# First two chunk pairs of a state-space scan in half chunks of 64 tokens, and the loads and row products that go with it

## The chip, the cores and the metric

The kernel runs on one core of one Trainium2 chip. The metric is the device time of an execution in microseconds, smaller being better. TensorE (PE) multiplies matrices, VectorE (DVE), ScalarE (ACT) and GpSimd (POOL) do the elementwise work, SyncE (SP) issues nearly all transfers. PE's weight loads are listed apart as PEld, the queue of an engine's issued transfers with a q (SPq).

## The reference

A Mamba-2 scan (batch 4, 8 heads, 768 tokens, head size D = 32, state size N = 16) is followed by a two-layer block with a PReLU. In exact arithmetic the chunk length doesn't matter, and the kernel chooses its own.

```
for each chunk of the sequence:
    cum = cumsum(log a);  L[i, j] = exp(cum_i - cum_j), i >= j
    y = ((C B^T) * L) x  +  (C state) * exp(cum)
    state = exp(sum log a) * state + sum_j exp(cum_end - cum_j) B_j x_j
x2 = y as (3072 tokens, 256)
h = x2 @ w_in                                  # 256 x 2048
g = max(h, 0) + alpha * min(h, 0)
out = g @ w_out                                # 2048 x 256
```

`w_in` and `w_out` come as 64-bit floats, all else as 32-bit floats.

## The kernel before

**Tiling.** A pair `gp` is two chunks of 128 tokens of one batch row with all 8 heads: twelve pairs, three to a batch row. Four chunks (two pairs) are a group of 512 tokens, `xts[g]`, on which the two layers work. Group 0 is special: `first_two` runs pairs 0 and 1, then `hidden_two(0, f, t0, hp)` multiplies blocks f and f+1 of w_in by one half of the group's tokens, and from f = 4 on a loop runs `hidden(0, f)`, `output(f - 4)` and the steps of the next pairs (`ssm(2)`, `ssm(3)`), each a stage of the generator `pair(gp)`. The later groups run in `quad` and the like; nothing in them is changed.

**Weights.** They come in pieces of 512 KB (`raw`), in the order w_in 0, 1, 2, w_out 0, w_in 3, w_out 1, w_in 4, w_out 2, and so on in turn. Each is converted in four steps: `convert_a` (ACT twice, then POOL `wt` L267), `sign` (DVE L286), `convert_b` (DVE L296) and the add on POOL (L318). `convert_next` ends the conversion of the next piece and issues the load of the piece that is six further: the three calls in `first_two` issue pieces 6, 7 and 8.

**Pairs 0 and 1 before.** The decays of a chunk are made by a scan: PE spreads a row of `a` over 128 partitions (`spread_rows` L499, `spread` L511), DVE scans it against an identity (L908, L855), and the product with the gram of B and C (`gram_of` L822, `times` L851, on DVE or, through a copy by ACT, on POOL) is the weight by which x is multiplied (`outputs`, L870 and L878). `added` (L831) makes a chunk's contribution to the state, the state follows on DVE (L937, L968), `mask` on POOL (L838) spreads it for PE. `xT` is copied out of PSUM by ACT (L883).

**Row products.** `a` of half the batch is loaded as 96 rows of 128 tokens. `rows_scan` makes the products from each token to the chunk's end, `rows_turn` turns them over on PE for `pair_loads` (bn), `rows_out` stores the clamped rows (`z`) and the running products (`pf`) in DRAM. `ap` of a pair is loaded back from `pf` with each row repeated over partitions (L177, L223). Pair 2's state (L613) and its cd (L653, POOL) read pair 2's `ap`; its scans (L538) read `abc`, which is loaded from `z` (L160).

**Order.** It is written out by hand: `tc.manual_schedule` names all five engines, and each takes its instructions, SP its transfers, in the order of the program. A transfer's consumer, and a later transfer that reads what it stored, waits for its semaphore.

Of the kernel before, what the change touches and what calls it, by code (L numbers as in the profile page):

```python
# [9 lines left out]
F32 = mybir.dt.float32  # L10
# [12 lines left out]
def kernel(  # L23
# [25 lines left out]
    nc = tc.nc  # L49
# [112 lines left out]

    def load_pair(gp, decays=True):
# [8 lines left out]
        if gp == 0:  # L172
            load_a(ap, b, c)
        elif gp >= NB:
            rows = scratch["pf", b // 2].rearrange("(b h c) t -> b h (c t)", b=2, h=H)
            rows = rows[b % 2, :, c * Q : (c + 2) * Q]
            nc.sync.dma_start(out=ap, in_=rows.unsqueeze(1).to_broadcast([H, N, 2 * Q]))  # L177
# [42 lines left out]
    def load_second():  # L220

        rows = scratch["pf", 0].rearrange("(b h c) t -> b h (c t)", b=2, h=H)
        nc.sync.dma_start(out=loads["p", 1][3], in_=rows[0, :, 2 * Q : 4 * Q].unsqueeze(1)  # L223
                          .to_broadcast([H, N, 2 * Q]))
# [98 lines left out]
    def keep_warm(to, n, cols=2 * Q):  # L323

        for i in range(n):
# [6 lines left out]
    ident_h = const.tile([P, H * Q], F32, name="ident_h")  # L332
    nc.vector.tensor_copy(out=ident_h.rearrange("p (h t) -> p h t", h=H),
                          in_=ident.unsqueeze(1).to_broadcast([P, H, Q]))
# [17 lines left out]
    nc.vector.memset(ends[:, Q - 1 :], 1.0)  # L352

# [35 lines left out]
    def identity_bank():  # L389


        m5_bank.append(bank(3))
        nc.scalar.copy(out=m5_bank[0][:, HT:], in_=ident_h[:, :HT])
        ident_p.append(m5_bank[0][:, HT:])
# [15 lines left out]

    def rows_clamp(i):
        rows = loads.pop(("r", i))
        d0 = prep.tile([RW, SQ], F32, name="r0")
        nc.vector.tensor_scalar(out=d0[:, :Q], in0=rows, scalar1=1e-6, scalar2=1.0,
                                op0=ALU.max, op1=ALU.min)
        if i:
            nc.vector.tensor_scalar(out=d0[:, Q + 1 :], in0=rows[:, HQ + 1 :], scalar1=1e-6,
                                    scalar2=1.0, op0=ALU.max, op1=ALU.min)
        held[i] = d0
# [11 lines left out]
    def rows_out(i):  # L431


        d0 = held.pop(i)[:, : SQ if i else Q]
# [7 lines left out]

    def rows_turn(i, pr):

        ps = ss_tile() if i else ps_s.tile([P, 512], F32, name="ss")
        nc.tensor.transpose(ps[:, :RW], pr, ident[:RW, :RW])
        if i == 0:
            nc.tensor.transpose(ps[:, RW : RW + NF], al_n, ident[:NF, :NF])
        else:
            nc.tensor.transpose(ps[:, RW : 2 * RW], held["prs"], ident[:RW, :RW])  # L450
        t = bat.tile([P, RW], F32, name="prt")
        if i == 0:
            nc.scalar.copy(out=t, in_=ps[:, :RW])
        for v in range(2 if i else 0):
# [6 lines left out]
        if i == 0:  # L461
# [3 lines left out]
    def pair_loads(gp):  # L465
# [8 lines left out]
        else:  # L474
            pj = prt[i].rearrange("p (b h c) -> p b c h", b=2, h=H)[:, bi, c : c + 2]
# [6 lines left out]
    def first_a(ap, eng):  # L482

        z = prep.tile([P, 2, Q], F32, name="z", bufs=2)
        eng.memset(z[:, :, :1], 0.0)
        eng.tensor_scalar(out=z[:, :, 1:], in0=ap.rearrange("p (k t) -> p k t", k=2)[:, :, 1:],
                          scalar1=1e-6, scalar2=1.0, op0=ALU.max, op1=ALU.min)
        return z

    def spread_rows(z):  # L490

        ts = [bank(r) for r in range(4)]
        for k in range(2):
            for e in range(2):
                for r in range(4):
                    rs = slice(32 * r, 32 * r + 32)
                    row = 32 * r + N * e
                    cs = slice((2 * k + e) * Q, (2 * k + e + 1) * Q)
                    nc.tensor.matmul(ts[r][:, cs], ident[rs, row : row + 1].to_broadcast([32, P]),  # L499
                                     z[rs, k], start=(k == 0 and e == 0), stop=True,  # L500
                                     tile_position=(32 * r, 0), skip_group_check=True)
        return ts

    def spread(z, k, tile=lambda w: ss_tile()):

        ts = [tile(w) for w in range(2)]
        for q in range(4):
            for w in range(2):
                rs = slice(64 * w, 64 * w + 64)
                row = 64 * w + N * q  # L510
                nc.tensor.matmul(ts[w][:, q * Q : (q + 1) * Q],  # L511
                                 ident[rs, row : row + 1].to_broadcast([64, P]), z[rs, k],
                                 start=(q == 0), stop=True, tile_position=(64 * w, 0),
                                 skip_group_check=True)
        return ts
# [276 lines left out]
    def first_two():  # L792


        nat0, _, xt0, ap0 = loads["p", 0]

        dec = [work.tile([P, 2, H, Q], F32, name="dec") for i in range(2)]
        first = dec[0].rearrange("p a b t -> p (a b t)").rearrange(
            "p (r c) -> p r c", r=4)
        by_bank = first.rearrange("p r (k e t) -> p r k e t", k=2, e=2)  # L800
        pf0 = prep.tile([P, Q], F32, name="pf")
        new = {}

        def turned(nat, tp):
# [5 lines left out]
            nc.scalar.copy(out=bc.rearrange("p i t -> p (i t)"), in_=tp)  # L810
            cz = czp.tile([P, 2, 2, Q], F32, name="cz")
            for e in range(2):
                nc.scalar.mul(cz[:, e].rearrange("p k t -> p (k t)"),
                              bc[:, 2:].rearrange("p k t -> p (k t)"), par[:, e : e + 1])
            return bc, cz

        def gram_of(bc, cz, banks):
            gram = [t.rearrange("p (k h t) -> p k h t", k=2, h=2) for t in banks]
            for k in range(2):
                for r in range(4):  # L820
                    rs = slice(32 * r, 32 * r + 32)
                    nc.tensor.matmul(gram[r][:, k].rearrange("p h t -> p (h t)"), bc[rs, k],  # L822
                                     cz[rs, :, k], start=True, stop=True,
                                     tile_position=(32 * r, 0), skip_group_check=True)
            return gram

        def added(dps, bn, xt):
            for k in range(2):
                for r in range(4):
                    rs = slice(32 * r, 32 * r + 32)  # L830
                    nc.tensor.matmul(dps[rs, k], bn[:, k, rs],  # L831
                                     xt[:, k, 2 * r * D : 2 * (r + 1) * D],
                                     start=True, stop=True, tile_position=(0, 32 * r),
                                     skip_group_check=True)

        def mask(sm, new, ks):
            n = ks.stop - ks.start
            nc.gpsimd.tensor_tensor(  # L838
                out=sm.rearrange("p k (g m) -> p k g m", g=2),
                in0=new[:, ks].unsqueeze(2).to_broadcast([P, n, 2, 2 * D]),  # L840
# [3 lines left out]
        def copied(gram):  # L844
            g0 = op.tile([P, GT], F32, name="o_sb").rearrange("p (k h t) -> p k h t", k=2, h=2)
            nc.scalar.copy(out=g0, in_=gram)
            return g0

        def times(i, r, gram, eng=nc.vector):
            o = dec[1][:, :, 2 * r : 2 * r + 2] if i else by_bank[:, r]  # L850
            eng.tensor_tensor(out=o, in0=gram, in1=o, op=ALU.mult)  # L851

        def decays(k, w, t):
            ws = slice(512 * w, 512 * w + 512)
            nc.vector.tensor_tensor_scan(out=dec[1][:, k].rearrange("p h t -> p (h t)")[:, ws],  # L855
                                         data0=t, data1=ident_h[:, ws], initial=0.0,
                                         op0=ALU.mult, op1=ALU.add)

        def outputs(i, tiles, st, cd, xt, ws, warm=0):
            y = [t[:, : 2 * Q].rearrange("p (k t) -> p k t", k=2) for t in tiles]  # L860
            keep_warm(y[ws[0]].rearrange("p k t -> p (k t)"), warm)
            begun = False
            for k in range(2):
                if st[k] is None:
                    continue
                for q in range(4):
                    qs = slice(32 * q, 32 * q + 32)
                    for w in range(KC):
                        hs = slice(64 * w, 64 * w + 64)
                        nc.tensor.matmul(y[w][qs, k], st[k][hs, qs], cd[hs, k],  # L870
                                         start=not begun, stop=False,
                                         tile_position=(64 * w, 32 * q), skip_group_check=True)
                begun = True
            for w in ws:
                for k in range(2):
                    for q in range(4):
                        h = 4 * w + q
                        nc.tensor.matmul(y[w][32 * q : 32 * q + 32, k],  # L878
                                         xt[:, k, h * D : (h + 1) * D],
                                         dec[1][:, k, h] if i else by_bank[:, h // 2, k, h % 2],  # L880
                                         start=False, stop=True, tile_position=(0, 32 * q),
                                         skip_group_check=True)
                nc.scalar.copy(out=xts[0][:, w, 2 * i * Q : 2 * (i + 1) * Q],  # L883
                               in_=y[w].rearrange("p k t -> p (k t)"))

        def bn_of(gp):
# [585 lines left out]
```

## Time and profile before

| what | us |
|---|---|
| median of 3 runs | 358.47 (358.37 to 358.62) |
| the profiled execution | 358.36, its span 356.6 |
| first matmul of `hidden_two(0, 0, 0)` | 17.74 |
| first matmul of `hidden_two(0, 0, 2 * Q)` | 24.76 |
| `hidden(0, 4)` | 28.69 |
| PE busy | 349.9 (98%) |
| DVE, ACT, POOL busy | 240.4, 174.1, 205.3 |

The profile is one execution; its times count from the span's start. In a line of a timeline stand the start, the length, the engine, the line of the kernel, the instruction, output and inputs, the shapes, and in brackets how long the engine had been idle before and what ended that. The chain lists what the end waited for, in order of time.

### The profile page before, as it was taken

To read this page: it belongs to the slowest core of one execution; us is meant where nothing else is said; L and a number is where in the kernel's file an instruction comes from. 1 tells how busy PE (TensorE), PEld (TensorE's weight loads), DVE (VectorE), ACT (ScalarE), POOL (GpSimd) and SP (SyncE) were. 2 spreads that over 40 slices of the span, in tenths; PEclk is the share of its full clock that TensorE was granted. 3 is DMA by queue.
4 is the path that set the end of the run, shared out by engine and by line. 5 is a ranking of instruction groups with operands and counts; after the bars stand their busy time and mean duration, and the time that the engine had idled before them with its cause. 6 is when DMAs were issued, how large, how long until landed. Compare 5 with 4: busy or idle time off the path is not lost.

```text
span 356.6 us, 7560 instructions
## 1 busy us (share of the span) xinstructions
PE 349.9 (98%) x2894; PEld 288.3 (81%) x2894; DVE 240.4 (67%) x467; ACT 174.1 (49%) x387; POOL 205.3 (58%) x221
## 2 busy tenths in 40 slices
PE   8799999999999999999999999999999999999995
PEld 7576666578888888888888888888888888888885
DVE  6988986998748856857747856757856633643463
ACT  3577666535355346345345445345445344443431
POOL 4887568589938855725646626637526535434520
PEclk9999999999999999999999999999999999999999
DMA  7999999408355404403513513522001002002102
GB/s 115 188 195 328 289 249 226 121 16 167 93 96 124 98 2 75 104 2 75 94 41 74 91 48 68 92 51 61 13 4 29 0 2 31 0 0 32 29 1 62
DMA packets 105469, 30.19 MB, mean 85 GB/s; under 512 B 79880, under 2 KB 101336, under 8 KB 105432
## 3 DMA queue, kind: packets, MB, share of 16 engines
q1 hardware_dynamic: 105048, 29.52, 38.2%
q8 instruction: 23, 0.38, 0.4%
q10 hardware_dynamic: 384, 0.18, 0.2%
q14 instruction: 14, 0.11, 0.1%
HBM read 26.32 MB, written 3.37 MB: 83 GB/s over the span
## 4 chain that ended last, share of the span: by engine, by line
PE 95%; POOL 1%; DMA 1%; SPq 1%; issue 0%; ACT 0%; DVE 0%; POOLq 0%
PE bank L1108 33%; PE hp L1133 29%; PE bank L1034 8%; PE hp L996 6%; PE ss L1133 6%; PE hp L1011 2%; PE ss L758 1%; PE ss L702 1%; PE bank L1101 1%; PE ss L750 1%; DMA nat<-in_C_dram 1%; PE ss L776 1%; PE ss L713 1%; PE bank L511 1%; PE ss L589 1%; PE ss L768 0%
## 5 line engine op out<-in xcount | busy, mean ns | idle before, releaser
L1190 POOL TENSOR_TENSOR gt<-gt 128x512 f32<-128x512 f32 x58 | 74.1, 1278 | 21.1 <-DVE gt L1118 16.3
L1108 PE MATMUL bank<-gt,w_out 128*128 128x256 f32 x320 | 83.5, 381 | 0.0
L1108 PEld LDWEIGHTS bank<-gt,w_out 128*128 128x128 f32 x320 | 60.1, 190 | 9.2 <-issue 1.0
L1118 DVE SCALAR_TENSOR_TENSOR gt<-hp,s_mul,gt 128x256 f32<-128x256 f32 x96 | 42.0, 479 | 29.1 <-ACT gt L1116 26.9
L1180 POOL TENSOR_TENSOR gt<-gt 128x512 f32<-128x512 f32 x20 | 25.4, 1269 | 62.7 <-DVE gt L1118 56.0
L1116 ACT ACTIVATE gt<-hp,s_alpha 128x256 f32<-128x256 f32 x96 | 40.4, 472 | 34.5 <-PE hp L1133 31.4
L1108 PE MATMUL bank<-gt,ws 128*128 128x256 f32 x224 | 55.9, 379 | 0.0
L1108 PEld LDWEIGHTS bank<-gt,ws 128*128 128x128 f32 x224 | 42.3, 190 | 5.6
L1133 PE MATMUL hp<-xs,w_in 128*128 128x256 f32 x160 | 41.9, 384 | 0.0
L1133 PE MATMUL hp<-xs,ws 128*128 128x256 f32 x160 | 41.2, 380 | 0.0
L1159 DVE TENSOR_TENSOR hp<-hp,u 128x512 f32<-128x512 f32 x20 | 14.0, 700 | 35.2 <-ACT u L1157 35.2
L1133 PEld LDWEIGHTS hp<-xs,ws 128*128 128x128 f32 x160 | 30.3, 190 | 4.3 <-POOL xs L1075 0.2
L1133 PEld LDWEIGHTS hp<-xs,w_in 128*128 128x128 f32 x160 | 29.7, 190 | 4.5
L1034 PE MATMUL bank<-w_out,gt 128*128 128x256 f32 x128 | 31.0, 384 | 0.0
L1034 PEld LDWEIGHTS bank<-w_out,gt 128*128 128x128 f32 x128 | 23.6, 190 | 6.5 <-issue 2.9
L1133 PE MATMUL ss<-xT,w_in 128*128 128x256 f32 x96 | 24.6, 379 | 0.0
L996 PE MATMUL hp<-xT,w_in 128*128 128x512 f32 x48 | 22.7, 596 | 0.1
L616 POOL TENSOR_TENSOR sm<-state,bmask 128x256 f32<-128x256 f32 (+1 forms) x10 | 6.2, 618 | 28.9 <-DVE state L613 28.9
L532 DVE TENSOR_TENSOR_SCAN dec<-abc,bank 128x192 f32<-128x192 f32 x48 | 22.7, 523 | 0.0
L1148 ACT COPY m<-hp 128x512 f32<-128x512 f32 x8 | 4.7, 587 | 35.7 <-PE hp L1133 35.7
L1157 ACT COPY u<-hp 128x512 f32<-128x512 f32 x20 | 11.7, 586 | 19.4 <-PE hp L1133 19.4
L1167 DVE TENSOR_TENSOR c<-hp,m 128x512 f32<-128x512 f32 x20 | 13.8, 691 | 10.0 <-PE hp L1133 9.9
(204 smaller groups left out, 624.7 us busy)
## 6 DMA issues: line engine op xcount, KB each, us to landing
abc<-z SPq DMA_DIRECT2D x24, 192.0 KB
raw<-in_moe_w_in_dram SPq DMA_DIRECT2D x8, 512.0 KB
raw<-in_moe_w_out_dram SPq DMA_DIRECT2D x8, 512.0 KB
abc<-z SPq DMA_DIRECT2D x8, 512.0 KB
out_dram<-o_sb SPq DMA_DIRECT2D x32, 64.0 KB
nat<-in_B_dram SPq DMA_DIRECT2D x26, 64.0 KB
nat<-in_C_dram SPq DMA_DIRECT2D x24, 64.0 KB
xt<-in_x_dram SPq DMA_DIRECT2D x12, 128.0 KB
```

The lines of the kernel that those rows point to most:

```text
L532: nc.vector.tensor_tensor_scan(out=dv[:, o : o + SQ], data0=abc[k][:, s : s + SQ], data1=ident_p[0][:, :SQ], initial=0.0, op0=ALU.mult, op ...
L996: nc.tensor.matmul(hp, w_in[:, k, f * P : (f + 1) * P], xts[g][:, k], start=(k == 0), stop=(k == KC - 1))
L1034: nc.tensor.matmul(pos[0][t // 2][:, t % 2], gt[:, t * Q : (t + 1) * Q], w_out[:, f], start=(f == 0 and t % 2 == 0), stop=(f == NF - 1), s ...
L1108: nc.tensor.matmul(ms[g][i][:, h], w, blocks[g, z][n][:, p], start=(q == 0 and h == 0), stop=(q == NQ - 1), skip_group_check=True)
L1116: nc.scalar.mul(o[:, p], h[:, p], s_alpha[:, fs[p]])
L1118: nc.vector.scalar_tensor_tensor(out=o[:, p], in0=h[:, p], scalar=s_mul[:, fs[p]], in1=o[:, p], op0=ALU.mult, op1=ALU.max)
L1133: nc.tensor.matmul(to[:, p], w(2 * z + p), b, start=start and p == 0, stop=True, skip_group_check=True)
L1157: nc.scalar.copy(out=u2, in_=A)
L1159: nc.vector.tensor_tensor(out=Y, in0=Y, in1=u2, op=ALU.add)
L1167: nc.vector.tensor_tensor(out=c22, in0=A, in1=m5, op=ALU.add)
L1180: nc.gpsimd.tensor_tensor(out=tc_, in0=g22, in1=g12, op=ALU.subtract)
L1190: eng.tensor_tensor(out=o, in0=x0, in1=x1, op=ALU.subtract)
```

## The change

Pairs 0 and 1 are handled as four chunks of 64 tokens each, two to a half of the partitions, so the scans and products are over 256 elements and not 512, with tiles of 32x64 on PE. A chunk's state is made and masked one at a time. Pair 1's steps are put among the matmuls of `hidden_two(0, 2, 0)` by a function that is called after each. The copies out of y go half to ACT and half to DVE. A set of row products for chunks of 64 (`rows_short`) is made first and stored as `short`, from which pair 1's `ap` comes. The products for chunks of 128 come at the end of `first_two` (`rows_scan`, `rows_products`, then `load_products` of pair 2's `ap`, then `rows_turn`), and `load_pair(2)` no longer loads that `ap`. The `z` store, with its clamps now on POOL, follows pair 1's loads.

```diff
+    def load_products(gp, ap):
+        b, c = divmod(2 * gp, CPB)
+        rows = scratch["pf", b // 2].rearrange("(b h c) t -> b h (c t)", b=2, h=H)
+        rows = rows[b % 2, :, c * Q : (c + 2) * Q]
+        nc.sync.dma_start(out=ap, in_=rows.unsqueeze(1).to_broadcast([H, N, 2 * Q]))
     def load_pair(gp, decays=True):
...
-        elif gp >= NB:
-            rows = scratch["pf", b // 2].rearrange("(b h c) t -> b h (c t)", b=2, h=H)
-            rows = rows[b % 2, :, c * Q : (c + 2) * Q]
-            nc.sync.dma_start(out=ap, in_=rows.unsqueeze(1).to_broadcast([H, N, 2 * Q]))
+        elif gp > NB:
+            load_products(gp, ap)
...
     def load_second():
-        rows = scratch["pf", 0].rearrange("(b h c) t -> b h (c t)", b=2, h=H)
+        rows = scratch["short", 0].rearrange("(b h c) t -> b h (c t)", b=2, h=H)
...
+    def clamp(eng, out, in_):
+        eng.tensor_scalar(out=out, in0=in_, scalar1=1e-6, scalar2=1.0, op0=ALU.max, op1=ALU.min)
+    def rows_products():
+        d0 = held.pop(0)
+        rpf = prep.tile([RW, Q], F32, name="rpf")
+        nc.vector.tensor_tensor_scan(out=rpf, data0=d0[:, :Q], data1=zeros[:RW], initial=1.0,
+                                     op0=ALU.mult, op1=ALU.add)
+        scratch["pf", 0] = dr.tile([RW, Q], F32, name="pf0")
+        nc.sync.dma_start(out=scratch["pf", 0], in_=rpf)
...
+    def rows_short(r, rows):
+        clamp(nc.vector, starts_r[:RW, ::HQ], rows[:, ::HQ])
+        nc.vector.memset(r[:, ::HQ], 0.0)
+        pr = lent[3][:RW, 2]
+        nc.vector.tensor_tensor_scan(out=pr[:, ::-1], data0=r[:, 1:][:, ::-1],
+                                     data1=ends_q[:RW, ::-1], initial=0.0, op0=ALU.mult,
+                                     op1=ALU.add)
+        rpf = lent[3][:RW, 3]
+        nc.vector.tensor_tensor_scan(out=rpf, data0=r[:, :Q], data1=starts_r[:RW], initial=0.0,
+                                     op0=ALU.mult, op1=ALU.add)
...
     def first_two():
...
+        def spread(z, ts):
+            for e in range(2):
+                for r in range(4):
+                    rs = slice(32 * r, 32 * r + 32)
+                    row = 32 * r + N * e
+                    for j, hs in enumerate(halves):
+                        o = ts[r][hs, : 2 * Q].rearrange("p (k e t) -> p k e t", k=2, e=2)
+                        nc.tensor.matmul(o[:, :, e], ident[rs, row : row + 1]
+                                         .to_broadcast([32, HQ]), z[rs, :, hs], start=e == 0,
+                                         stop=True, tile_position=(32 * r, HQ * j),
+                                         skip_group_check=True)
+        def scan(i, r, t):
+            nc.vector.tensor_tensor_scan(out=dec[i][:, r], data0=t[:, : 2 * Q], data1=ident_q,
+                                         initial=0.0, op0=ALU.mult, op1=ALU.add)
...
+        def times(i, r, t):
+            nc.vector.tensor_tensor(out=dec[i][:, r], in0=t[:, 2 * Q :], in1=dec[i][:, r],
+                                    op=ALU.mult)
...
+        def copy_out(i, y):
+            for w in range(KC):
+                o = xts[0][:, w, 2 * i * Q : 2 * (i + 1) * Q].rearrange(
+                    "p (k j t) -> p j k t", k=2, j=2)
+                nc.scalar.copy(out=o[:, 0], in_=y[w][0])
+                nc.vector.tensor_copy(out=o[:, 1], in_=y[w][1])
...
+        nc.sync.dma_start(out=scratch["short", 0], in_=held.pop("short"))
         load_pair(1)
         load_second()
...
+        rows_clamp(0)
+        rows_out(0)
         load_next(2)
         load_pair(2, False)
         load_next(2)
         load_spread(2, *divmod(4, CPB))
...
+        convert_next()
+        convert_a(*pieces[1])
         xts[0] = xtp.tile([P, KC, GT], F32, name="xT")
+        copy_out(0, y)
+        sign(*pieces[1])
+        convert_b(*pieces[1])
+        prelu_of = {0: hidden_two(0, 0, 0, spare())}
+        for r in range(4):
+            scan(1, r, sp[r])
+        bn1 = pair_loads(1)
         convert_next(first=False)
+        mask(0, slice(3, 4))
+        own = [ss(), ss()]
+        bc1, cz1 = turned(nat1, own[0], nc.scalar)
...
+        added(dps, bn1, xt1)
+        cd1 = decayed_c(bc1, pf1)
+        def among(i, k):
+            if (i, k) == (0, 1):
+                states(1, dps, pf1)
+                gram_of(bc1, cz1, sp)
+                one_at_a_time(1, range(3))
+                for r in range(4):
+                    times(1, r, sp[r])
+                prelu_of[0]()
+                convert_a(*pieces[2])
+                sign(*pieces[2])
+            if (i, k) == (1, 0):
+                y = places(own, [bank(0), bank(1)])
+                x_products(y, xt1, 1)
+                state_products(y, 1, cd1)
+                copy_out(1, y)
+        prelu_of[2] = hidden_two(0, 2, 0, spare(), among)
+        convert_next(first=False)
+        mask(1, slice(3, 4))
         slope_signs()
+        prelu_of[2]()
+        pr = rows_scan(0)
+        rows_products()
+        load_products(NB, loads["p", NB][3])
+        rows_turn(0, pr)
```

In `hidden_two` the ACT part of the PReLU (L1017) moves into the function that it returns where t0 is 0.

## The prediction

> **What bounds the kernel now.** I read the busy tenths in 40 slices first, then the chain that ended last in order of time, then the timeline from 0 to 56 us engine by engine, SyncE's queue (SPq) included.
>
> ```profile
> PE   8799999999999999999999999999999999999995
> DVE  6988986998748856857747856757856633643463
> DMA  7999999408355404403513513522001002002102
> ```
>
> TensorE (PE) is full from the third slice on, so a microsecond won or lost in front of it is won or lost at the end, unless PE waits somewhere later. The DMA engines are full in the first seven slices, to about 60 us, and VectorE (DVE) nearly so. The chain says where the full stretch starts:
>
> ```profile
> 24.33 0.38 ACT xT L883
> 24.71 0.04 issue
> 24.76 3.80 PE hp L1011 x16
> 28.56 0.13 issue
> 28.69 1.95 PE hp L996 x4
> ```
>
> At 24.76 pair 1's xT lies in SBUF and the two `hidden_two(0, ..., 2 * Q)` start; from there no link but PE follows. All that the change does in front counts by how it moves 24.76, called T1. All that it moves behind T1 counts by what it makes PE wait for. Three places of the timeline show how little room there is behind T1: SPq, DVE, and the conversion of w_out that `output(4)` needs.
>
> ```profile
> 31.84 0.41 SPq L249 DMA_DIRECT2D raw<-in_moe_w_in_dram  x1
> 32.36 0.41 SPq L249 DMA_DIRECT2D raw<-in_moe_w_out_dram  x1
> ```
> ```profile
> 35.29 0.75 DVE L1000 SCALAR_TENSOR_TENSOR gt<-hp,s_mul,gt 128x512 f32<-128x512 f32 x1
> 35.95 0.27 DVE L613 SCALAR_TENSOR_TENSOR state<-state,ap,ss 128x64 f32<-128x64 f32 x1
> 36.14 2.41 DVE L538 TENSOR_TENSOR_SCAN dec<-abc,bank 128x256 f32<-128x256 f32 x4
> ...
> 44.22 0.69 DVE L296 SCALAR_TENSOR_TENSOR wr<-wt,wr 128x512 uint32<-128x512 uint32 x1
> ```
> ```profile
> 45.00 1.27 POOL L318 TENSOR_TENSOR w_out<-wr,wg 128x512 uint32<-128x512 uint32 x1 [1.16 <-DVE wr L296]
> ...
> 46.41 1.90 PE L1034 MATMUL bank<-w_out,gt 128*128 128x256 f32 x8
> ```
>
> L613 is pair 2's state and reads `ap`, the products of pair 2. Today `ap` is loaded at 17.15, so L613 never waits. From L613 to L296 at 44.22 DVE has no gap over 0.2 us; GpSimd (POOL) waits for that L296, and PE takes the result 0.14 us after POOL's 46.27. So a delay of L613 reaches PE at `output(4)`, less some 0.1 us.
>
> **What the Trainium skill says.** "PSUM — Partial Sum Buffer", section "Engine vs sequencer instructions": the queues of ScalarE, VectorE and GpSimd are strict FIFO; a late L613 holds all behind it. The trace agrees: starts follow the program's order. "DMA: Bandwidth & Descriptors", section "Two DMAs through the same engine are not ordered": a transfer that reads what another wrote must be issued after a wait for the first one's semaphore, so the issuing queue stands. The same page, "Anatomy of one DMA", gives a fixed part of about 2.0 us, most of it the receipt of the last byte. Here: issued into an idle queue, the first `ap` took from 0.79 to 3.73, when DVE used it, 2.9 us; raw piece 1 had its last packet at 12.52 and ScalarE (ACT) began it at 13.25, 0.7 us later. "TensorEngine Tiling (Array Packing)", section "Available Configurations": 32x64 tiles are eight at once. The later half pairs agree: L702's 64 records ran in 0.84 us, while L713's 32x128 tiles took 1.08.
>
> **The front, part by part.** The setup (two 64x256 identity copies for one of 128x1024 at 0.77, four memsets) lies beside `keep_warm`, which holds PE to 4.58 while z is done at 4.07; without that cover it costs up to 0.5. The store `short` is ready on DVE at about 5.3 and SPq comes to it at 7.5; `load_second` waits for its landing near 13.5, and SPq is there at 15; the z store needs POOL's clamps, done by 9.5. So SPq stands nowhere new in front. DVE: eight scans of 512 (4.57 us at L908, 4.8 at L855) become eight of 256 at 0.60 (L538), -4.6. The products with the gram, five on DVE at 0.68 and three on POOL (1.28, 1.77, 1.29) with ACT copies of 0.59, become eight on DVE at 0.35 (half of 0.68): DVE -0.6, POOL -4.3, ACT -1.8. Added on DVE: four more L968-like states at 0.28 (1.1), two more row scans (0.42 + 0.40), four copies out of y at about 0.25 (half of an ACT 0.37, plus start). Added on POOL: masks one by one at 0.46 to 0.63 (eight instructions against three, +2.5) and three row clamps, 1.2 by L486's 1.06 for 254 elements. PE: spreads 1.59 and 2.06 become about 0.9 and 0.65, each gram 1.1 becomes 0.65; `added` at L589's 0.45 is level.
>
> Pair 0, in order: spread done at 5.6; scans to 8.0; cz and pf0 on DVE to 8.9; gram done at 9.2; products and states to 11.7; POOL's three masks end at 11.8. Then w_in piece 0: ACT 11.3 to 12.0, POOL 12.6, DVE 13.3, POOL's add (1.27) 14.6. `copy_out` stands on ACT behind `convert_a` of piece 1, whose data comes at 13.25 as today: 13.25 + 0.68 + 0.67 + 2 x 0.28 = 15.15. So the first `hidden_two` starts at **15.2 instead of 17.74**.
>
> Pair 1: `hidden_two` 1.95 and transposes 0.65 to 17.8; ACT's four copies (0.37, 0.45, 0.45, 0.37) to 19.5; `added` to 18.7 (xt's last packet is at 17.13); two matmuls of the next `hidden_two`, then gram at 20.3. POOL: cd (0.73) 20.3, three masks 22.1. DVE: products 20.3 to 21.7. So the state products end at 22.6, `hidden_two` at 23.1, xT is ready by 23.6: 1.2 before T1. But `rows_turn(0)` stands on PE before the next `hidden_two`, and its `pr` comes from a DVE scan behind `convert_b` (to 24.3), two `rest` (0.44 each, to 25.2), a memset and the scan (0.48): 25.6, and **T1 becomes about 25.9, +1.1 us**. Its uncertainty is about -2.5 to +1 us, since each engine's order was worked out by hand. Without that transpose T1 would be 23.4, -1.4.
>
> **The products of pair 2.** This is what I expect to decide. `ap` of pair 2 leaves SPq at 17.15 and comes back at the end of `first_two`, behind a store of `pf`. Ahead of that store on SPq stand the raw loads of the three `convert_next`: pieces 6, 7, 8, of 512 KB, issued at 27.41 to 32.25. In the trace's DMA packets the queue is served in that order: abc of pair 2, then piece 6 from 32.97, piece 8's last packet at 37.50. The early `ap` falls out (its packets lay among nat's from 20.79), -0.4: 37.1. Then:
> - `pf`'s 96 packets: 0.2, 37.3.
> - Its receipt, a store to DRAM, which no row shows: not under the 0.7 of a load, hardly over the skill's 2.0; I take 1.0, 38.3. SPq stands from 32.3 on; behind it wait pieces 9 to 11 and pair 3's loads.
> - `ap`: 0.6 us of issue, landing 2.9 to 3.3 after its start. The lower is the first `ap`; for the upper, another `ap` into an idle queue was issued at 79.06 with its last packet at 81.41, plus 0.7 to 1. **41.4**, between 40.4 and 42.6.
>
> L613 waits for it: 41.4 against 35.95 (36 to 37 with T1 moved), so DVE is 5.5 us behind today. Nothing takes it up: behind L613 come 9.0 us of work to L296's end at 44.91, and DVE is full. POOL stands too: cd (L653) reads `ap`. PE: the gram of pair 2 needs a bank that L1000 (39.59) frees, now at 45.8 instead of 40.3; `output(4)` needs POOL's add, at 51.7 instead of 46.27. PE is delayed by 5.5 - 0.1 to 0.2 = 5.3. The front's +1.1 or -1.4 is **contained in this, not added**: PE waits there until a time that the transfers set. The later pieces come some 3 us later, which a PE 5.3 later doesn't feel.
>
> The sum is made against 358.36, the profiled execution (span 356.6 and 1.7 around it), 0.11 below the median of 358.47: 358.4 + 5.3 = **363.7**. With the landing's bounds: +4.3 to +6.5. If DVE or POOL catch up by up to 2 us (L286 took 0.41 to 1.35, longer beside POOL), +2.5.
>
> **Rivals.**
> - *The products come in time and the front gains*: what decides is whether `ap` lands before 36. For it: rows_products is done at 26, far ahead of need. Against: three pieces ahead in the queue. With T1 at 23.4, PE starts 1.4 earlier and the later conversions move with it: 357.0; between 356 and 358.
> - *The products come in time, but `rows_turn` holds PE*: +1.1, 359.5. It speaks for it that `pr` comes last on DVE. Point of decision: the scan later than 23.4.
> - *The change doesn't shorten the front*, because piece 1's landing at 13.25 and POOL's conversions bound it anyway: T1 as today, 358.4, if `ap` were in time. I count this with the second.
>
> **How the numbers follow.** The stall by pair 2's products 0.78; products in time with a gain 0.14; in time with a loss or none 0.08. From 359.0 to 366.0 lie 0.95 of the first and about 0.7 of the last, 0.8 together. A difference of 0.2% (0.7 us) is about what a measurement of this kernel can tell. Faster by over that: nearly all of the gain case, 0.14; within: 0.03; slower: 0.83.
>
> **What would show it.** Right: `ap` from `pf` on SPq with a wait of several us in front; pair 2's state on DVE with an idle of 3 to 5 us before it that a DMA ends, at about 41; PE idle between 43 and 52; the first `hidden_two` near 15. If that state waits for no DMA, the main step is wrong. If PE idles before `rows_turn`'s transpose near 23 to 25, the second rival's mechanism is there; if `hidden_two(0, 0, 2 * Q)` starts before 24, it isn't.

## The result, and the profile after

The changed kernel takes **364.93 us** (median of 6 runs, 364.25 to 365.31) against 358.42 (357.96 to 358.62) for the kernel before, measured beside it: a ratio of 1.0182 [1.0168, 1.0195], **6.5 us slower**. The profiled execution took 365.23, its span is 362.4, so span against span it is 5.8 us. PE is busy for 353.2 us, 3.3 more than before.

The busy tenths of the page, 9 us to a slice:

```profile
PE   8869999999999999999999999999999999999996
DVE  7874795989846756766656866657866634743363
DMA  7889689704535510510540530530201001001102
```

The string of PE now has a 6 in its third slice and is full only from the fourth on, while DVE's has a 7 and a 4 in slices 3 and 4, where it had two 8s. The chain of waits shows two stations in that stretch that the kernel before did not have (start, length, engine, tile, line):

```profile
24.06 0.64 PE hp L1088 x2
24.73 0.85 ACT gt L1098 x2
25.60 0.88 DVE gt L1109 x2
26.52 0.43 DVE pr L457
26.95 0.14 issue
27.08 0.39 PE ss L497
27.48 3.48 PE hp L1088 x8
...
33.28 6.17 DMA pf<-rpf
39.46 2.86 DMA ap<-pf
...
42.41 0.28 DVE state L637
...
50.98 1.28 POOL w_out L322
...
52.31 1.78 PE bank L1120 x7
```

First station: PE's transpose in `rows_turn` (L497) waits for the scan `pr` (L457), which comes behind ACT's and DVE's share of the PReLU. Second: pair 2's state (L637) waits for its products, which wait for their own store. The last two lines are the add on POOL that `output(4)` waits for and `output(4)` itself, at 52.31 where it stood at 46.41. That is +5.9, and the span ends 5.8 later: PE's lateness there is carried to the end.

The stretches in figures (stretch, length, busy us of PE, PEld, DVE, ACT, POOL with their counts, then granted clock, DMA share, GB/s), the changed kernel first, then the kernel before:

```profile
24.70:27.30 2.60, 0.22 (x2) 0.25 (x2) 2.14 (x6) 0.84 (x2) 1.93 (x2) 0.81 0.83 100
27.30:33.70 6.40, 6.40 (x18) 5.16 (x18) 2.04 (x5) 2.66 (x6) 1.49 (x4) 0.54 0.99 305
```
```profile
24.76:28.66 3.90, 3.80 (x16) 2.79 (x17) 3.41 (x7) 2.89 (x7) 2.19 (x3) 1.00 1.08 226
```

Read them from the left: between 24.7 and 27.3 PE worked 0.22 us. Then it did in 6.4 us what had taken 3.9, without a gap, and the reason stands in the clock's column: 0.54 instead of 1.00. The clock's record in the trace has TensorE at half its clock from 26.31 to 33.14. So `hidden(0, 4)` starts at 33.66 instead of 28.69, 5.0 us late, before pair 2's products matter at all.

SPq's timeline, for the second station, and the state on DVE:

```profile
32.77 0.41 SPq L253 DMA_DIRECT2D raw<-in_moe_w_in_dram  x1
33.28 0.41 SPq L437 DMA_DIRECT2D pf<-rpf  x1
39.46 0.60 SPq L167 DMA_DIRECT2D ap<-pf  x1
40.17 0.40 SPq L253 DMA_DIRECT2D raw<-in_moe_w_out_dram  x1
```
```profile
42.41 0.28 DVE L637 SCALAR_TENSOR_TENSOR state<-gt,ap,ss 128x64 f32<-128x64 f32 x1 [1.49 <-DMA ap<-pf]
```

The store `pf` follows piece 8 at once; its load follows 6.2 us later, and everything behind it on SPq as well. The bracket of L637 says how much of this DVE felt: 1.49 us only, because DVE was late for the first reason already. PE felt it as a single wait, at `output(4)`:

```profile
52.31 1.99 PE L1120 MATMUL bank<-w_out,gt 128*128 128x256 f32 x8 [0.44 <-POOL w_out L322]
```

PE was 5.0 us late at `hidden(0, 4)`, still 5.0 at `output(3)` (47.91, 42.87 before), and 5.9 at `output(4)`. So 5.0 of the 5.9 us had been lost in the front, and the products added at most the last 0.9.

### The profile page after: what moved, and what is told of

Read it like the earlier page. It is cut to its first block, busy times and chain, and to the rows that moved or that the text cites. A ratio compares the mean times of both kernels' runs of the same rounds, so it can differ in the third digit from the quotient of the medians.

```text
span 362.4 us, 7825 instructions
## 1 busy us (share of the span) xinstructions
PE 353.2 (97%) x3011; PEld 290.5 (80%) x3011; DVE 238.7 (66%) x487; ACT 171.3 (47%) x386; POOL 203.5 (56%) x226
## 4 chain that ended last, share of the span: by engine, by line
PE 87%; DVE 4%; DMA 4%; SPq 2%; POOL 1%; ACT 1%; issue 1%; DVEq 0%; POOLq 0%
PE bank L1194 33%; PE hp L1219 28%; PE bank L1120 6%; PE ss L1219 6%; PE hp L1073 3%; DMA pf<-rpf 2%; PE hp L1088 2%; PE ss L782 1%; DVE dec L562 1%; DMA raw<-in_moe_w_in_dram 1%; PE ss L726 1%; PE bank L1187 1%; PE ss L774 1%; DVE wr L300 1%; PE ss L800 1%; DMA ap<-pf 1%
## 5 line engine op out<-in xcount | busy, mean ns | idle before, releaser
L1120 PEld LDWEIGHTS bank<-w_out,gt 128*128 128x128 f32 x128 | 23.6, 190 | 7.2 <-issue 3.1
L1204 DVE SCALAR_TENSOR_TENSOR gt<-c,s_mul,gt 128x256 f32<-128x256 f32 x40 | 20.6, 555 | 0.0
```

The lines of the kernel that those rows point to most:

```text
L1120: nc.tensor.matmul(pos[0][t // 2][:, t % 2], gt[:, t * Q : (t + 1) * Q], w_out[:, f], start=(f == 0 and t % 2 == 0), stop=(f == NF - 1), s ...
L1204: nc.vector.scalar_tensor_tensor(out=o[:, p], in0=h[:, p], scalar=s_mul[:, fs[p]], in1=o[:, p], op0=ALU.mult, op1=ALU.max)
```

## The experiments

Two causes overlap, so the question was which of them sets the end. My theory: the later of the two does, the products in the changed kernel (42.4, then `output(4)`), with the front close behind; taking away either alone gives little. The first rival: the front is all, and the products' wait is a shadow of it. The second: the products are all, and the front costs its predicted +1.1.

### The front's wait alone taken away: `turn_late`

```diff
-        rows_turn(0, pr)
+        held["pr0"] = pr
...
     identity_bank()
+    rows_turn(0, held["pr0"])
```

> Only rows_turn(0) is moved, from before hidden_two(0, 0, 2 * Q) to after identity_bank(). Theory: PE's delay is the larger of two, not their sum: the front (wait for pr and slow clock, +5.0 at hidden(0, 4)) and pair 2's ap (state at 42.4, +5.9 at output(4)). Without the wait hidden_two(0, 0, 2 * Q) starts at 24.7 to 24.9 and hidden(0, 4) at 28.7 as in the kernel before, but pair 2's state still comes at 42 to 42.6, so the time stays at 364.0 to 365.2. Rival, the front makes the loss and ap only its last 0.9: 359.0 to 359.6.

Measured: 364.92 us, 1.0177 [1.0149, 1.0205]. The second half's `hidden_two` started near 25.1 and not at 27.3. Three of its waits between 24 and 75 us (who waited for whom: us in all, times, longest):

```profile
PE hp L1073 <- DVE gt L1109: 2.3, 1, 2.3
DVE state L637 <- DMA ap<-pf: 2.2, 1, 2.2
PE bank L1120 <- POOL w_out L322: 0.4, 1, 0.4
```

PE met a new wait at `hidden(0, 4)`, which came at 31.33, before the 33.66 of the changed kernel but not at the 28.7 that was expected. What is late there can be read from the timelines of ACT and POOL:

```profile
28.43 1.12 ACT L279 ACTIVATE wg<-raw,g_add,g_mul 128x256 f32<-128x256 uint16 x2 [1.89 <-POOL g_add L391]
29.46 1.55 ACT L1098 ACTIVATE gt<-hp,s_alpha 128x256 f32<-128x256 f32 x4
```

ACT's conversion of piece 3 needs `g_add`, which `slope_signs` leaves on POOL behind piece 2's add, and the PReLU stands behind it on ACT. The edit therefore traded 2.4 us for 2.3 and was followed by half a clock again (31.18 to 34.60). Even so it tells: `hidden(0, 4)` was 2.3 us earlier, `output(4)` came at 52.36 (52.31 without the edit). A front 2.3 us better brings nothing while pair 2's state stands at 42.46.

### The products by another queue: `ap_early`, `ap_early_warm`, `both`

In all three, the store of `pf` and the load of `ap` are issued by ACT's queue, not SP's. `ap_early_warm` adds six `keep_warm` matmuls ahead of `rows_turn`; `both` has the late `rows_turn` of the first experiment as well.

```diff
...
-        nc.sync.dma_start(out=scratch["pf", 0], in_=rpf)
+        nc.scalar.dma_start(out=scratch["pf", 0], in_=rpf)
...
-        load_products(NB, loads["p", NB][3])
...
     convert_a(*pieces[4])
+    load_products(NB, loads["p", NB][3], nc.scalar)
```

> pf is stored from ACT's queue and pair 2's ap is loaded from ACT's queue after convert_a of piece 4, so that neither stands behind pieces 6 to 8; rows_turn stays where it is. Theory (the larger of two): pair 2's state waits for no transfer, what is left is the front with hidden(0, 4) at 33.7: 363.2 to 364.2. Rival, ap makes all of the loss and the front is covered: 358.0 to 359.5.

> As ap_early, and six matmuls of 256 columns on ones (2.3 us) are put on PE before rows_turn(0), in the time in which PE waits for pr. Theory: the wait of 2.6 us stays, but the granted clock stays at 1.00, so the two hidden_two take 3.9 us and not 6.2: hidden(0, 4) at 31.2 to 31.6, time 360.8 to 361.8. Rival, the clock falls for another reason than PE's idling, or its fall costs nothing: as ap_early, 363.2 to 364.2.

> turn_late and ap_early together. Theory: both causes are gone, and nothing else in the change costs time: hidden_two(0, 0, 2 * Q) at 24.7 to 24.9, pair 2's state at 36 without a wait, time 358.0 to 358.8, as the kernel before. Rival, a third cause among the new parts (more copies and masks, smaller tiles): over 359.3. If the first hidden_two at 15.2 were worth its 2.5 us: 356.

Measured: `ap_early` 363.71, 1.0145 [1.0121, 1.0169]; `ap_early_warm` 363.31, 1.0142 [1.0123, 1.0162]; `both` 364.69, 1.0166 [1.0141, 1.0191]. **The edit did not do what it was for.** The chain of `ap_early_warm`:

```profile
27.87 5.87 DMA pf<-rpf
...
33.77 7.11 DMA ap<-pf
...
40.97 0.28 DVE state L637
```

The store was issued five us earlier and its first packet ran at 32.17, 4.3 us after; the load's first packet ran at 37.79, 4.0 us after. At the start of the changed kernel, with the DMA engines idle, a load of as many bytes on ACT's queue was issued at 0.80 and had its first packet at 1.82, 1.0 us after. So the queue itself isn't that slow: here a queue of its own didn't get past DMA engines that the pieces and `abc` held (busy to 0.91 from 27.9 to 32.2). These runs therefore can't take the products' delay away, and that is the main reason why `ap_early_warm` and `both` missed their ranges. `ap_early` lies inside its range, but by luck: its state was to wait for no transfer and waited 1.6 us for `ap`. `both` shows in addition that late steps find each other: its `hidden(0, 4)` waited 2.9 us for the PReLU behind `slope_signs` and then ran on half a clock:

```profile
33.69 0.14 issue
33.83 3.04 PE hp L1072 x4
```

Two things can be kept. The first is what sets `output(4)`. In the changed kernel, `turn_late`, `ap_early` and `ap_early_warm` the wait for POOL there is 0.4 us, and `output(4)` follows pair 2's state by 9.9 us in each: state at 42.41, 42.46, 42.79 and 40.97, `output(4)` at 52.31, 52.36, 52.68 and 50.86. Their `hidden(0, 4)` lay at 33.66, 31.33, 33.38 and 31.94. So the state, and with it `ap`, is what ends last there, wherever the front stands within these bounds.

The second concerns the clock. In the profile of `ap_early_warm` it stayed at 1.0 up to the end, but this can't be put down to the filler, since in that of `ap_early` it didn't fall at this place either. PE stood as long as in the changed kernel, and the sixteen matmuls behind ran at full clock:

```profile
28.70 0.27 PE L497 MATMUL ss<-ident,pr 96*128 96x96 f32 x1 [2.39 <-DVE pr L457]
28.81 3.65 PE L1087 MATMUL hp<-xT,w_in 128*128 128x256 f32 x16
```

The one slow stretch of `ap_early` before its end came from 16.82 to 20.23, after PE had stood 2.0 us near 13.

### The products in time: `ap_on_time`, `ap_on_time_warm`

Here the scan and the store of `pf` come straight after the store of `z`, as in the kernel before, and `ap` is loaded just ahead of its `abc`. The front is left as it is; the second kernel alone has the line with `keep_warm`, six matmuls (twelve instructions in the trace, 2.8 us) that fill PE's gap.

```diff
         rows_out(0)
+        rows_products()
         load_next(2)
         load_pair(2, False)
         load_next(2)
+        load_products(NB, loads["p", NB][3])
...
         pr = rows_scan(0)
-        rows_products()
-        load_products(NB, loads["p", NB][3])
+        keep_warm(own[0][:, : 2 * Q], 6)
         rows_turn(0, pr)
```

> The pf scan and store follow the z store (SP at about 16), and pair 2's ap is loaded just ahead of its abc, so both stand in front of pieces 6 to 8; rows_turn(0) stays before hidden_two(0, 0, 2 * Q). Theory (PE's delay is the larger of the front and ap): pair 2's state waits for no transfer, the front's wait for pr and its slow clock stay, hidden(0, 4) at 33.4 to 34: 363.0 to 364.0. Rival, ap makes all of the loss: 358.4 to 359.4.

> As ap_on_time with six matmuls on ones before rows_turn(0). Theory: the wait stays, the clock does not fall; hidden(0, 4) at 31.2 to 32.0: 361.0 to 362.0. Rival, the slow clock costs nothing of its own: as ap_on_time.

Measured: `ap_on_time` 363.02, 1.0126 [1.0098, 1.0154], that is +4.7; `ap_on_time_warm` 361.98, 1.0093 [1.0063, 1.0122], +3.6. Pair 2's state waited for no transfer in either (40.26 and 38.84). The one wait of PE over 0.2 us that is left from 24 us on in the first, and the stretch in its chain:

```profile
PE ss L497 <- DVE pr L457: 2.4, 1, 2.4
```
```profile
27.73 0.27 PE ss L497
28.00 5.17 PE hp L1088 x16
33.17 1.72 PE hp L1073 x4
```

The sixteen matmuls took 5.2 us for 3.8 (half clock from 28.41 to 31.82). An earlier stretch at half the clock, from 14.75 to 18.17, came after a stand of 1.2 us near 13. With the products in time the rest of the change, nearly all of it the front, costs +4.7 **alone**. That refutes the second rival: the front isn't worth +1.1. It also bears on the first: the late products add 1.8 us to what the front costs.

In the profiled execution of the kernel with the filler no stretch is at half the clock before the end, and the sixteen matmuls took 3.6 us. Of the +4.7 the median loses 1.0; 3.6 stays. That isn't a clean price of the clock: the other three executions had mean clocks of 0.989 to 0.995, against 0.998 in the profiled one, and took 361.60 to 362.99 us against its 361.01.

### The products late, and nothing else: `before_ap_late`

The kernel before, with the early load of pair 2's `ap` left out and in its place a second store of the same products and a load from it, where the changed kernel has them.

```diff
-        elif gp >= NB:
+        elif gp > NB:
...
+        held["rpf"] = rpf
...
         outputs(1, (bank(0), bank(1)), (sm0[1][:, 0], sm1[:, 0]), cd1, xt1, (0, 1))
+        scratch["late", 0] = dr.tile([RW, Q], F32, name="late0")
+        nc.sync.dma_start(out=scratch["late", 0], in_=held["rpf"])
...
+        nc.sync.dma_start(out=loads["p", 2][3], in_=rows[0, :, 4 * Q : 6 * Q].unsqueeze(1)
+                          .to_broadcast([H, N, 2 * Q]))
```

> The kernel before with one part of the change alone: pair 2's ap is loaded at the end of first_two, after a second store of the same pf rows, behind pieces 6 to 8; the early store stays for pair 1. Theory: pair 2's state waits until about 42 and nothing takes it up: 363.5 to 365.0, as much as the whole change. Rival, the wait is covered by PE's own queue of work: 358.4 to 359.4.

Measured: 366.34, 1.0216 [1.0182, 1.025], **+8.0**, more than the whole change. DVE's longest wait and the chain:

```profile
DVE state L614 <- DMA ap<-late: 7.2, 1, 7.2
```
```profile
32.83 7.72 DMA late<-rpf
...
40.57 2.76 DMA ap<-late
...
43.84 0.28 DVE state L614
```

The state moved from 35.95 to 43.84, 7.9 us. PE stood 3.2 and 1.8 us at pair 2's gram. This refutes the first rival: the products need no late front to cost that much. The size was missed (363.5 to 365.0 expected) because the store took 7.7 us and because PE, left without work, then ran at half its clock from 44.52 to 54.76.

### Everything late cleared: `front_cleared`

`ap_on_time`, with `rows_turn` behind `identity_bank` and `slope_signs` ahead of piece 2's add.

```diff
         prelu_of[2] = hidden_two(0, 2, 0, spare(), among)
+        slope_signs()
         convert_next(first=False)
         mask(1, slice(3, 4))
-        slope_signs()
         prelu_of[2]()
         pr = rows_scan(0)
-        rows_turn(0, pr)
+        held["pr0"] = pr
...
     identity_bank()
+    rows_turn(0, held["pr0"])
```

> As ap_on_time, with rows_turn(0) after identity_bank() and slope_signs() on POOL before the conversion of piece 2 (with rows_turn late it had become the next wait: hidden(0, 4) stood 2.3 us for a PReLU behind ACT's wait for g_add). Theory: all three waits are gone, hidden(0, 4) at 28.4 to 29.2: 358.0 to 359.0, level with the kernel before. Rival, the instruction stream: PE stands 1 to 2 us at 12.9 for nothing the profile shows, and if that decides, 359.5 to 361. If the early first hidden_two is worth its 2.5: 356.

Measured: 359.35, 1.0029 [1.0017, 1.0041], +1.0. This misses the range of 358.0 to 359.0 by 0.35 and stays just under the rival's 359.5. Three moved steps take back 5.5 of the 6.5 us. `hidden(0, 4)` was at 29.58, 0.9 behind the kernel before. In the timeline of PE there is a gap that nothing in the profile explains, after which the first `hidden_two` ran at half the clock and took 2.76 us for 1.9:

```profile
14.31 0.96 PE L859 MATMUL bank<-gt,ident 32*64 32x128 f32 x24 [1.08 <-issue]
15.20 1.22 PE L330 MATMUL bank<-const-float32-1.0 128*128 128x128 f32 x4
16.21 2.76 PE L1088 MATMUL hp<-xT,w_in 128*128 128x256 f32 x8
```

### Pair 1's steps pulled forward: `turned_first`, `turned_first_b`

What remained was the question where the 2.5 us went by which the first `hidden_two` is earlier. In `front_cleared` ACT stood for 4.6 us until `turned(nat1)` had run behind that `hidden_two`. So pair 1's transposes go ahead of it, and its gram, states, masks and products with the gram straight behind, no longer inside `among`. `turned_first_b` has the x and state products after the last part, (1, 1), of the second `hidden_two`.

```diff
+        own = [ss(), ss()]
+        bc1, cz1 = turned(nat1, own[0], nc.scalar)
         prelu_of = {0: hidden_two(0, 0, 0, spare())}
...
+        gram_of(bc1, cz1, sp)
...
         added(dps, bn1, xt1)
+        states(1, dps, pf1)
+        one_at_a_time(1, range(3))
...
             if (i, k) == (1, 0):
                 y = places(own, [bank(0), bank(1)])
```

> Built on front_cleared: pair 1's B and C are turned over on PE ahead of the first hidden_two, where ACT stood idle for 4.6 us, and its gram, added and states follow straight behind it; x products after the third part of hidden_two(0, 2, 0). Theory (the early first hidden_two is lost on the chain turned, ACT copies, gram, products, state products): the second half's hidden_two moves from about 25.1 to about 23.9, hidden(0, 4) from 29.6 to 28.4 or 28.7, and the time is 358.0 to 358.8, level with or just under the kernel before. Rival (DVE's scans and POOL's conversion of piece 2, whose data lands at 21.6, bound the front): hidden(0, 4) stays at or after 29.2 and the time at 359.0 to 359.8.

> The same with the x and state products after the last part of hidden_two(0, 2, 0), so that PE doesn't wait for DVE's products in the middle of it. Theory: 357.8 to 358.6. If the second half's hidden_two is bound by when xT is copied, PE waits some 0.6 us there instead and the time is that of turned_first within 0.3 us. Rival: 359.0 to 359.8 as for turned_first.

Measured: 359.49, 1.0027 [1.0019, 1.0036], and 359.4, 1.0017 [1.0007, 1.0028]; the kernel before had 358.54 in that session. `turned_first` missed its range of 358.0 to 358.8 by 0.7, `turned_first_b` its 357.8 to 358.6 by 0.8; both lie in the middle of the rival's 359.0 to 359.8. The starts moved (`hidden(0, 4)` at 29.07 and 28.82, 28.69 in the kernel before), but in `turned_first_b` the second half's `hidden_two` only got to 24.92. Its chain says why:

```profile
14.02 0.98 POOL w_in L322
...
15.37 0.68 POOL wt L271
16.07 0.69 DVE wr L300
16.77 2.35 DVE dec L865 x4
19.16 0.65 PE bank L874 x20
20.20 1.92 PE hp L1086 x8
22.12 0.63 PE ss L921 x32
22.75 0.66 PE bank L921 x32
...
24.50 0.28 DVE xT L942
...
24.92 3.69 PE hp L1086 x16
```

Pair 1's scans (L865) stand on DVE behind the conversion of piece 1 (L300), which stands behind POOL's two steps; the gram waits for the scans. The first `hidden_two` starts 2.0 us earlier than in the kernel before (15.75, 17.74), the gram ends 1.4 earlier (19.81, 21.17), and the eight matmuls behind it end 1.0 earlier (22.12, 23.09). That last lead goes in the x and state products (L921, then eight steps of L933), 2.4 us from 22.12 to 24.51, where the kernel before needs 1.2:

```profile
23.09 0.60 PE bank L870 x32
23.69 0.62 PE bank L878 x16
```

So 0.6 of the lead is lost on the chain through DVE, 0.4 on `added`, which now stands between the gram and those matmuls, and 1.1 on the new form of the x and state products. In the profile of `turned_first` one more loss follows: `hidden(0, 4)` is 0.4 late but `output(4)` 1.3 (47.73), after DVE had waited 1.35 us, until 31.79, for a raw piece. No kernel of this study beats the kernel before.

## Why the prediction was right

Forecast 363.7 with a range of 359.0 to 366.0 and slower at 0.83; measured 364.93. The path that it named, from `pf` through `ap`, pair 2's state and POOL's add to `output(4)`, is the one that ended last. But its signs came only in part. `ap` left SPq after 6.2 us of waiting for its store, and the first `hidden_two` started near 15, as forecast. Pair 2's state, though, stood 1.49 us for the transfer and not 3 to 5, and PE stood 0.44 us between 43 and 52, where nearly all of the loss was to fall. The step that failed is the front, put at +1.1: it cost 5.0 us before the products met PE. The total hides this, because the two overlap; and it couldn't have told them apart, since the front alone (363.02) lies in the forecast's range too. By its steps:

**The products: right, nearly in every term.** The claim was that `pf`'s packets follow those of pieces 6 to 8 and not its own issue. In the trace of the changed kernel's DMA packets the three pieces end at 38.85 and `pf`'s lie from 37.55 to 39.05. The pieces had been put at 37.1: 1.75 early, since SPq issued the last of them 0.4 later and the packets ran longer. The receipt, set to 1.0, was at most 0.4 (last packet at 39.05, load issued at 39.46), so that error and the first partly cancel. `ap` took 2.86 (2.9 predicted). State at 42.41 (41.4), the end of POOL's add at 52.26 (51.7). "DMA: Bandwidth & Descriptors" of the Trainium skill, section "Anatomy of one DMA", lays most of its fixed 2.0 us on the receipt, and describes transfers that GpSimd issues; this store was issued by SP, and of its 6.2 us at least 5.8 had passed when its last packet ran. `before_ap_late` shows that this step suffices alone, and that in the kernel before it costs 8.0 and not 5.3: the state came at 43.84, and the slow clock behind PE's stand, which the forecast has no term for, came on top.

**The front: right in its mechanism, mis-sized.** The first `hidden_two` started at 15.26, as predicted (15.2), and `rows_turn` held PE for `pr`, as the second rival had it. But T1 was 27.3 and not 25.9, and what followed took 6.4 us and not 3.9. Three terms failed:
- *The state products*, set to end 0.5 after the masks (22.1 to 22.6), took 1.06 (23.0 to 24.06), eight steps of about 0.1 us one behind the other, and the gram took 1.04 for 0.65.
- *A wait that I hadn't seen*: pair 1's `dps` lies in a bank that a scan still reads, so `added` waited 0.9 us for DVE's fourth scan (18.66). With these, `hidden_two` ended at 24.69 (23.1 predicted) and the scan at 26.94 (25.6).
- *The clock.* I let PE stand without asking what it costs afterwards. PE stood 2.4 us, and the matmuls behind took 2.5 more than before, at half the clock.

**"Contained, not added": right.** With the front alone at +4.7 and the products alone at +8.0, a sum would have been +12.7; the change costs 6.5. Both delays run beside each other up to `output(4)`. That the front's term was 3.9 us too small at `hidden(0, 4)` moved the total little for this reason. Nor is it simply the larger of the two: in `before_ap_late` PE has run ahead, is then left without work and runs at half its clock for 10.2 us after; in the changed kernel it is held earlier and arrives later.

**The gain that did not come.** The rival with a gain puts T1 at 23.4 once `rows_turn` is out of the way (the forecast's own sum has xT ready at 23.6, so 23.4 is a slip of 0.2). `front_cleared` and `turned_first_b` put it at about 25.1 and 24.9. The 2.5 us at the first `hidden_two` are real and are lost again before T1: in `turned_first_b` about half goes by the end of the second `hidden_two`'s matmuls, mainly on piece 1's conversion and pair 1's scans, and half on x and state products that take 2.4 us for 1.2. The rival "the change doesn't shorten the front", with a time as before if `ap` were in time, is the nearest of the three once the other causes are cleared, with +0.6 to +1.0 measured (1.0017 to 1.0029).

**What stays open.** PE stood for 0.5 to 2.0 us near 13 in the kernels with the new front, without a wait that the profile names. In all ten of their traces a packet of an instruction queue ended 1.2 to 1.5 us before PE went on: at 12.28 in the one that went on first (13.56), at 14.01 in the one that went on last (15.22). That PE waited there for instructions that came late behind full DMA engines fits this, but no run tried it. How much of the remaining +0.6 to +1.0 comes from it is open too.

## What to carry to other kernels

A load that depends on a store costs the whole queue ahead of the store: count the bytes queued on all DMA engines, put the pair ahead of the large loads, and don't expect a second queue to overtake them (here ACT's didn't). When a step that is off the path is moved to the end of a stage, look for the in-order engine on which it now stands in front of the main work, as the transposes did on PE. And before a gain at the start of a stage is counted, follow it to the last instruction of that stage; here 2.5 us were gone 10 us later.

## What the runs showed of the hardware

A short stand of TensorE can cost about as much again, but not every time. "TensorE: Matmul & The Clock Gate" of the Trainium skill, Part 1, section "What's actually happening", gives half clock after at least one idle window of about 3.4 us. The length of the slow stretches agrees (3.41 us, 6.83, 10.24: one, two and three windows), but slow stretches came after shorter stands too, and the length of a stand alone doesn't decide:

| kernel | PE stood, us | half clock for, us |
|---|---|---|
| changed kernel | 2.39 | 6.83 |
| `ap_on_time` | 2.39 | 3.41 |
| `turn_late` | 2.33 | 3.41 |
| `ap_early` | 2.39 | none |
| `front_cleared` | 1.08 | 3.41 |
| `ap_on_time_warm` | 1.17 | none |

Each row is one profiled execution, and what decides isn't shown.

A store of 48 KB took 5.9 to 7.7 us in six kernels from issue to the point where its reader went on, on SP's queue and on ACT's, while the packets of other transfers held the DMA engines; its own packets ran for 1.2 to 2.1 us of that.
